# Threshold attention into a squared-ReLU MLP on one core: softmax reciprocals and divisions after the next step's maxima, one weight rounding moved a step, and the last weight block turned one step earlier

## The chip, the cores and the metric

The kernel runs as one launch on one core of a Trainium2 chip. The metric is the device time in microseconds (us), the median of several executions; the profile is of one further execution. The core has five queues that each run in program order: PE (matmuls; PEld is its weight loads), DVE (vector), ACT (scalar), POOL (GpSimd) and SP, which here only issues transfers. They meet through semaphores.

## The reference, cut to what matters

```python
# q, k, v: (8, 8, 576, 64) fp32; w_in (512, 2048), w_out (2048, 512); tau = 0.02
scores = q @ k.transpose(0, 1, 3, 2) / 8
thresh = scores.max(-1, keepdims=True) - tau
scores = np.where(scores >= thresh, scores, -1e9)
attn = np.exp(scores - scores.max(-1, keepdims=True))
attn = attn / (attn.sum(-1, keepdims=True) + 1e-9)
x = (attn @ v).transpose(0, 2, 1, 3).reshape(4608, 512)   # heads side by side
out = np.maximum(x @ w_in, 0) ** 2 @ w_out
```

## The kernel before

**Steps.** The attention is cut into 148 steps (`steps`, counted from 0; `NST` is 148, `END` is 150). A step is one block `i` of 128 query rows of one pair of heads (`vis`), and works on two heads `u` = 0, 1. The first four pairs have steps of two blocks each (steps 0 to 7), the next four of three blocks each (steps 8 to 19); the third block of those, `i` = 4, is a rest of 64 rows of both heads in one tile. A step consists of:

- *scores* on PE (L280, L273 for the rest), into four PSUM banks, two per head. The next step's scores reuse these banks, so they wait for L355 of the step before;
- *maxima* on DVE (L317), one per head;
- a bias and the exponentials on ACT (L331, L332, L335 in early steps; L340, L341, L343 later), into an SBUF tile `w`;
- *threshold* on DVE (L355): one scalar_tensor_tensor per head that compares the scores with the threshold, multiplies the exponentials by the result and leaves the row sum in `st`;
- a small reduction that bounds the sum from below and a *reciprocal* on DVE (L359, L360);
- *divide* on POOL (L365, then L367 per head): `w` times reciprocal;
- two steps later, `turn`: PE transposes `w` (L414, L421, L427) and ACT copies the result to `wT` (L415, L423, L428). From step 35 on DVE turns 32 x 32 blocks instead (`turn_blocks`, L459 to L469), and transfers place them: for each two blocks POOL issues one to DRAM (`set_aside`, L436, `aside`), and SP four from there into `wT` (L477);
- some steps after that, `mix`: PE multiplies `wT` by `v` (L530) and ACT copies the result to `xT` (L513 and its neighbours).

In between, DVE transposes the next keys and queries (`prep_part`, L254), and SP issues loads of q, k, v (L185, L188, L236).

**Early steps.** `early_to` is 11: steps 0 to 10 are written out by `early_step`. Steps 11 to 39 are in the main loop, steps 40 to 150 in `late_step`.

**Rounding of the MLP weights.** The weights arrive as 32 pieces (`weight_piece`), loaded by SP (L136) into three areas, and each is rounded in five stages by `round_weights(i, stage)`: stage 0 on ACT (L149, L150), stages 1 and 2 on DVE (L152, L154), stages 3 and 4 on POOL (L156, L158). `end_rounding` does stage 4, counts the piece in `state["rounded"]` and issues the load of the piece three further on. In the early steps a piece gets stage 0 in its own step (3, 5, 7, 8, 9) and the other stages in the next one: DVE's stages stand between L355 and L359, POOL's after the division. From step 11 on a piece has all its stages in its own step.

**MLP pieces.** When the first 256 tokens of `xT` are there, `add_chunk` puts the MLP's work into the queue `waiting`, in pieces of some 1.8 us of PE work (`PIECE_US`). `fill` takes pieces from it at four places of a step, at a rate that `rate` computes ahead. A piece may run if the number of rounded weight pieces that it needs is not over `state["usable"]`:

```python
state["usable"] = rounded_by[-1]          # the count at the start of the step before
rounded_by.append(state["rounded"])
```

The first chunk's first half is `mlp_in` (L579, four matmuls of 256 tokens, 8 PE instructions in the profile; relu and square by ACT L589 and DVE L591), its second half `mlp_out` (L764). `mlp_in` with `x` = 0 to 3 needs four rounded pieces. The first chunk is added in step 10. Later chunks use other products (L693, L799). All these decisions are made while the program is written down, so each queue's order is fixed.

**The end of the attention.** In `late_step` a step `s` turns the block of step `s` - 1. If that block's number is odd it does so right after its own maxima and exponentials (`first`), else behind its second `fill`. L816 is one of the additions that assemble the output of a chunk. Step 148 has no scores any more; it turns the block of step 147. The last `mix`, in step 150, needs what was turned, set aside and placed by then.

## Time and profile before

| What | us |
|---|---|
| median of three executions | 1318.65 (1318.54 to 1320.52) |
| the profiled execution | 1320.85 |
| its span, first to last instruction | 1319.1 |
| PE busy in the span | 1290.9 (98%) |
| DVE busy | 936.9 (71%) |
| POOL busy | 776.2 (59%) |
| ACT busy | 585.4 (44%) |

Three runs differ by up to 2.0 us, and the profiled one lies 2.2 us above their median. The page's busy time is a mean over parts that differ: up to about 200 us DVE is nearly as full as PE (9.8 of each 10 us from 70 to 110), later PE alone is full. PE's clock is granted at full speed almost everywhere (mean 0.997).

### The profile page before, as it was taken

The page shows a single profiled execution, that of the slowest core. Times are in us where ns is not written, and L with a number is a line of the kernel's source. Part 1 is how long each engine was busy: PE and PEld are TensorE (multiplying, and loading weights), DVE is VectorE, ACT ScalarE, POOL GpSimd, SP SyncE. Part 2 cuts the span into 40 slices and gives each one's busy share as a digit, 9 for nine tenths or more (in the row PEclk, how much of TensorE's full clock was granted, in tenths as well). Part 3 has the DMA queues.
Part 4 walks back from the last instruction along what each step waited for, and adds up shares of the span by engine and source line. Part 5 has one row for each costly group of instructions (what it writes and reads, how often), then busy time and mean ns, then how long its engine had stood idle before and what let it go on. Part 6 is the DMA issues. An engine that isn't in the chain of part 4 may idle for free.

```text
span 1319.1 us, 24730 instructions
## 1 busy us (share of the span) xinstructions
PE 1290.9 (98%) x8862; PEld 1070.6 (81%) x8862; DVE 936.9 (71%) x2034; ACT 585.4 (44%) x1353; POOL 776.2 (59%) x908
## 2 busy tenths in 40 slices
PE   7999999999999999999999999999999999999997
PEld 6676557897888888797978888888887988889997
DVE  6899776777777788788776877878686877522131
ACT  4887763244343526253435343525353434331331
POOL 3788874775747475556574746656574737455351
PEclk9999999999999999999999999999999999999999
DMA  6765431777777878686666768667676866520000
GB/s 127 156 181 145 126 73 60 145 173 168 165 173 178 181 177 186 143 200 160 170 157 158 158 154 187 172 137 185 146 173 139 198 162 161 144 53 9 9 17 17
DMA packets 320907, 185.48 MB, mean 141 GB/s; under 512 B 282224, under 2 KB 282256, under 8 KB 314384
## 3 DMA queue, kind: packets, MB, share of 16 engines
q1 hardware_dynamic: 309120, 115.78, 46.4%
q0 software_dynamic: 10000, 67.92, 12.9%
q8 instruction: 70, 1.15, 0.4%
q14 instruction: 53, 0.43, 0.1%
q10 hardware_dynamic: 1664, 0.21, 0.1%
HBM read 108.04 MB, written 68.42 MB: 134 GB/s over the span
## 4 chain that ended last, share of the span: by engine, by line
PE 83%; DVE 6%; DMA 3%; ACT 2%; issue 1%; POOL 1%; SPq 0%; DVEq 0%; POOLq 0%; ACTq 0%
PE big L693 29%; PE big L799 28%; PE big L530 10%; PE big L296 8%; PE big L579 3%; PE big L764 2%; PE big L280 2%; DVE st L317 1%; DMA wT<-aside 1%; DMA aside<-turned 1%; PE big L414 1%; DVE w L355 1%; ACT w L343 1%; DVE turned L154 0%; PE big L273 0%
## 5 line engine op out<-in xcount | busy, mean ns | idle before, releaser
L355 DVE SCALAR_TENSOR_TENSOR w<-big,st,w 128x576 f32<-128x576 f32 x269 | 207.4, 805 | 87.6 <-ACT w L343 85.6
L317 DVE TENSOR_REDUCE st<-big 128x1 f32<-128x576 f32 x288 | 204.1, 747 | 85.3 <-PE big L296 60.6
L367 POOL TENSOR_SCALAR w<-w,st 128x576 f32<-128x576 f32 x269 | 244.2, 916 | 29.4 <-DVE st L360 24.6
L799 PE MATMUL big<-wo,gsum 128*128 128x256 f32 x1088 | 243.8, 382 | 0.0
L799 PEld LDWEIGHTS big<-wo,gsum 128*128 128x128 f32 x1088 | 204.4, 190 | 37.0 <-issue 7.6
L693 PE MATMUL big<-xT,w_in_sb 128*128 128x128 f32 x1536 | 187.4, 277 | 1.5 <-DVE g L705 1.4
L693 PEld LDWEIGHTS big<-xT,w_in_sb 128*128 128x128 f32 x1536 | 178.5, 192 | 10.8 <-issue 7.7
L799 PE MATMUL big<-wo,g 128*128 128x256 f32 x816 | 185.3, 382 | 0.1
L343 ACT ACTIVATE w<-big,st 128x576 f32<-128x576 f32 x255 | 174.4, 735 | 0.2 <-issue 0.2
L799 PEld LDWEIGHTS big<-wo,g 128*128 128x128 f32 x816 | 151.6, 190 | 26.2 <-issue 6.5
L530 PE MATMUL big<-wT,vs 128*64 128x256 f32 (+5 forms) x1420 | 159.5, 389 | 4.9 <-DMA wT<-aside 3.5
L530 PEld LDWEIGHTS big<-wT,vs 128*64 128x64 f32 (+1 forms) x1420 | 86.0, 136 | 70.1 <-issue 20.8
L340 ACT ACTIVATE st<-st 128x2 f32<-128x2 f32 (+1 forms) x137 | 28.1, 205 | 253.3 <-DVE st L317 252.1
L365 POOL TENSOR_SCALAR st<-st 128x2 f32<-128x2 f32 (+1 forms) x148 | 35.6, 241 | 177.7 <-DVE w L355 167.1
L436 POOL DMA_DIRECT2D aside<-turned x50 | 29.9, 597 | 177.5 <-DVE turned L465 177.5
L705 DVE TENSOR_TENSOR g<-big,g 128x512 f32<-128x512 f32 x96 | 64.6, 676 | 83.7 <-PE big L693 78.1
L296 PE MATMUL big<-kT,qT 64*128 64x256 f32 (+3 forms) x768 | 107.0, 416 | 0.0
L296 PEld LDWEIGHTS big<-kT,qT 64*128 64x128 f32 x768 | 84.6, 186 | 14.5 <-issue 5.0
L701 ACT ACTIVATE g<-g 128x512 f32<-128x512 f32 x96 | 60.4, 630 | 63.5 <-DVE g L705 63.4
L569 POOL TENSOR_TENSOR gsum<-g 128x512 f32<-128x512 f32 x34 | 46.1, 1356 | 69.9 <-ACT g L702 69.6
L702 ACT ACTIVATE g<-g 128x512 f32<-128x512 f32 x128 | 80.9, 632 | 4.0
L459 DVE STREAM_TRANSPOSE turned<-w 128x512 f32<-128x512 f32 x100 | 70.2, 702 | 0.3 <-issue 0.3
(119 smaller groups left out, 2058.1 us busy)
## 6 DMA issues: line engine op xcount, KB each, us to landing
aside<-turned POOLq DMA_DIRECT2D x50, 1152.0 KB, 4.8
wT<-aside SPq DMA_DIRECT2D x200, 288.0 KB, 5.4
vs<-in_v_dram SPq DMA_DIRECT2D x72, 128.0 KB, 5.7
wo<-in_moe_w_in_dram SPq DMA_DIRECT2D x16, 512.0 KB, 4.8
wo<-in_moe_w_out_dram SPq DMA_DIRECT2D x16, 512.0 KB, 3.5
out_dram<-osb POOLq DMA_DIRECT2D x32, 256.0 KB, 3.9
kl<-in_k_dram SPq DMA_DIRECT2D x113, 72.0 KB, 2.8
ql<-in_q_dram SPq DMA_DIRECT2D x112, 72.0 KB, 5.7
```

Source lines behind the costliest of these rows:

```text
L296: nc.tensor.matmul(big[to, at + x0:at + x1], lhsT, keys[u * D:(u + 1) * D, x0:x1], start=True, stop=True)
L317: nc.vector.tensor_reduce(out=mx[:, u:u + 1], in_=sc[u], axis=AX.XY, op=ALU.max)
L343: nc.scalar.activation(out=w[:, u, :].rearrange("p (h k) -> p h k", h=2), in_=sc[u], func=AF.Exp, bias=bias[:, u:u + 1], scale=SCALE)
L355: nc.vector.scalar_tensor_tensor(out=wu, in0=sc[u], scalar=thr[:, u:u + 1], in1=wu, op0=ALU.is_ge, op1=ALU.mult, accum_out=sm[:, u:u + 1])
L367: nc.gpsimd.tensor_scalar(out=w[:, u, :], in0=w[:, u, :], scalar1=z[:, u:u + 1], scalar2=rcp[:, u:u + 1], op0=ALU.add, op1=ALU.mult)
L459: move(wb[:, 0:h, :, :], whole_[:, 0, :, :, :])
L530: nc.tensor.matmul(ps[u * D:(u + 1) * D, :], vs[n % 2][rows, u * (NBLK + 1) + c, :], wT[rows, at // REST:(at + ps.shape[1]) // REST, NBLK ...
L693: nc.tensor.matmul(to[:, f, :], factor(j, p, q, c)[:, f * P:(f + 1) * P], part[:, c, :], start=(p in "125" and f == 0 and c == 0), stop=(p ...
L701: nc.scalar.activation(out=to, in_=to if src is None else src, func=AF.Relu)
L702: nc.scalar.activation(out=to, in_=to, func=AF.Square)
L705: nc.vector.tensor_tensor(out=x, in0=to, in1=x, op=ALU.add)
L799: nc.tensor.matmul(to, left[:, f, :], wo[:, slot, f, :], start=(f == 0), stop=(f == HF - 1))
```

## The change

The reduction and the reciprocal become a function of their own, `reciprocals`. In the early steps from step 3 on `threshold` no longer calls it. The next step does, after its own maxima and exponentials: `finish_weights` issues the reciprocals, the division, and POOL's stages of the roundings whose DVE stages are done (kept in `turned_words`), with the loads that follow. Step 10 doesn't issue the DVE stages of the piece of step 9; step 11 does, after its maxima and after the reciprocal and the division of step 10. The DVE stages of step 11's own piece now both come after its threshold. In `late_step`, step 148 turns nothing more; step 147 turns the block of step 146 and then its own.

```diff
+    def reciprocals(vis, i):
+        st, n = weights[vis, i][2], len(weights[vis, i][1])
+        nc.vector.tensor_reduce(out=st[:, 5, 0:n], in_=st[:, 3:5, 0:n].rearrange("p j u -> p u j"), axis=AX.X, op=ALU.max)
+        nc.vector.reciprocal(st[:, 6, 0:n], st[:, 5, 0:n])
...
     def threshold(vis, i, between=()):
...
         for fn in between:
             fn()
-        nc.vector.tensor_reduce(out=den, in_=st[:, 3:5, 0:n].rearrange("p j u -> p u j"), axis=AX.X, op=ALU.max)
-        nc.vector.reciprocal(rcp, den)
+        if early() and state["step"] > 2:
+            return
+        reciprocals(vis, i)
...
     def late_step(s):
...
-        if first:
+        if first and s != NST:
             turn_last(s)
...
         if not first:
             some_later("vector")
             turn_last(s)
+            if s == NST - 1:
+                turn_last(NST)
...
+    def finish_weights(s):
+        reciprocals(*steps[s])
+        divide(*steps[s])
+        end_roundings()
+    def end_roundings():
+        while turned_words:
+            p = turned_words.popleft()
+            round_weights(p, 3)
+            end_rounding(p)
...
     def early_step(s):
...
         elif s > 2:
             scores(s)()
             early_exponents(n, i)
+        if s > 3:
+            finish_weights(s - 1)
...
-        threshold(n, i, [lambda p=p, x=x: round_weights(p, x) for p in rounding for x in (1, 2)])
-        divide(n, i)
-        while rounding:
-            p = rounding.popleft()
-            round_weights(p, 3)
-            end_rounding(p)
+        later_on = s == early_to - 1
+        threshold(n, i, [] if later_on else [lambda p=p, x=x: round_weights(p, x) for p in rounding for x in (1, 2)])
+        if not later_on:
+            turned_words.extend(rounding)
+            rounding.clear()
         rounding.extend(now)
+        if s < 3:
+            divide(n, i)
+            end_roundings()
...
     for s in range(END + 1):                      # the main loop, steps 11 to 39
...
             exponents(n, i)
+            if s == early_to:
+                finish_weights(s - 1)
+                while rounding:
+                    p = rounding.popleft()
+                    for x in (1, 2, 3):
+                        round_weights(p, x)
+                    end_rounding(p)
...
-            elif now:
+            elif now and s != early_to:
                 round_weights(now[0], 1)
...
-            if lay and now:
+            if now and (lay or s == early_to):
                 round_weights(now[0], 1)
```

## The prediction

> **What bounds the kernel now.** I read the page's engine rows, then the chain, then PE's idle times along the timeline, then the other engines at those places.

> ```profile
> PE 1290.9 (98%) x8862; PEld 1070.6 (81%) x8862; DVE 936.9 (71%) x2034; ACT 585.4 (44%) x1353; POOL 776.2 (59%) x908
> PE 83%; DVE 6%; DMA 3%; ACT 2%; issue 1%; POOL 1%; SPq 0%; DVEq 0%; POOLq 0%; ACTq 0%
> ```

> PE is busy 98% of the span. From about 60 us on its order runs nearly without holes, so the end moves only with PE's idle time after that, plus whatever the first 60 us gain or lose. Two stretches matter here.

> ```profile
> 34.26 0.82 DVE L355 SCALAR_TENSOR_TENSOR w<-big,st,w 128x576 f32<-128x576 f32 x1 [0.33 <-ACT st L331]
> 35.97 0.16 DVE L359 TENSOR_REDUCE st<-st 128x2 f32<-128x4 f32 x1
> 36.16 0.17 DVE L360 RECIPROCAL st<-st 128x2 f32<-128x2 f32 x1
> 36.41 1.61 DVE L317 TENSOR_REDUCE st<-big 128x1 f32<-128x576 f32 x2
> 37.94 0.77 DVE L254 STREAM_TRANSPOSE kT<-kl 128x576 f32<-128x576 f32 x1
> 38.70 0.82 DVE L355 SCALAR_TENSOR_TENSOR w<-big,st,w 128x576 f32<-128x576 f32 x1
> ...
> 58.96 1.24 PE L280 MATMUL big<-kT,qT 64*128 64x288 f32 x8 [1.76 <-DVE wo L355]
> 61.63 3.62 PE L579 MATMUL big<-xT,w_in_sb 128*128 128x256 f32 x16
> 65.18 1.24 PE L280 MATMUL big<-kT,qT 64*128 64x288 f32 x8
> ```

> (The timeline: start, length, engine, line, operation; in brackets the idle time before it and its releaser.) In the early steps DVE works almost without pause: two steps take 9.2 us, with 0.33 us lost to ACT. In step 11 (counted from 0) PE fills 61.63 to 65.25 with 16 instructions of L579, and the next scores follow at once. At the end of the attention part stands the last real PE hole:

> ```profile
> 1145.62 0.67 DVE L465 STREAM_TRANSPOSE turned<-w 128x512 f32<-128x512 f32 x1
> 1146.59 0.60 POOL L436 DMA_DIRECT2D aside<-turned  x1 [4.82 <-DVE turned L465]
> 1162.07 2.63 PE L530 MATMUL big<-wT,vs 128*64 128x256 f32 x24 [1.58 <-DMA wT<-aside]
> ```

> [...] L154 takes 0.43 us alone, but 1.39 us at 59.45, ending 0.28 us after POOL's L158 (59.21 to 60.56). [...] the granted clock is 0.51 from 18.0 to 21.5, and the 3.4 us before hold about 1.1 us of PE work.

> **The change part by part.** The number of instructions stays. I take the order of the built programs and walk it with the durations above.

> *Reciprocals and divisions moved (steps 3 to 10).* Reduction and reciprocal (L359, L360) cost 0.28 us of DVE issue (35.97 to 36.33, with the overlap into the next). They leave the place before the next maxima and come after them. In an odd step (5, 7) the maxima start 0.27 us earlier, because the roundings before them left the scores waiting; the pair then fills part of the 0.33 us that DVE waited for ACT: -0.27. In an even step (4, 6) no rounding stands before the maxima, so they already wait for PE (scores start 0.05 after L355 and need 1.23 us: 34.26 + 0.82 + 1.3 = 36.4, which is the start shown). Nothing is won there, while the pair now stands between maxima and the kT transpose, which led straight to L355 at 38.70: +0.28. Steps 8 and 9 start L355 when ACT is ready (ACT runs L149, L150 just before), so nothing moves. Sum to step 9: 0. Bounds: -0.8 if the even steps hide the pair, +0.9 if the odd steps gain nothing.

> [...] The division of step 8 now starts after the maxima of step 9, at 52.0 instead of 50.85, and POOL's roundings follow it: L156 at 53.6 to 54.9, L158 at 54.95 to 56.3 (before, 52.44 to 55.07). DVE's roundings of step 9 come at 54.45. Before they met only L158's tail (0.90 for L152). Now L152 meets L156 and L154 meets all of L158, ending near 56.6; the maxima of step 10 start at 56.5 instead of 56.00: +0.5. PE and ACT wait behind them. Bounds 0 and +1.3 (one whole L158).

> *Rounding of step 10's turn into step 11.* Its L152 and L154 (58.82 to 60.84) leave the place before the maxima of step 11, which then start about 60.7, when the scores are there, instead of 61.02. But reciprocal, L152 and L154 now precede L355[...]: L355 at 63.25 to 63.75 instead of 63.55. I take +0.1; bounds -0.3 to +0.2. SP: the loads L136 move behind loads of v and, in step 11, behind those of k and q; the piece needed at about 71 is issued near 64.5 and lands in 4.8 us (row of wo): no wait.

> *What the later rounding does to PE.* `rounded` is one piece behind (three instead of four when step 11 reads `usable`), so x = 0 of the first MLP chunk may not be placed in step 11. The built order shows it: step 11 loses both pieces (16 of L579), step 12 gets one more, step 16 the other. The order is equal again by step 17, apart from small shifts up to step 33. So PE stands idle in step 11 from about 62.3 to 65.1: a hole of 2.8 us, and the 3.46 us of work (16 x 0.216, their start distance) comes later. Step 12 repays 0.57 us (a hole before L427 in which the piece now lies), steps 13 and 16 0.22 and 0.75 (PE's waits for DVE at 76.1 and 93.5). Later holes of 1.03 and 0.62 (at 111.1 and 117.4) can repay more. Against that, pieces no longer lie between transposes in steps 17, 18, 20 and 21: there PE waits 0.41 or 0.57 for ACT's copies (as at 61.25 and 67.12), 1.96 if nothing covers it. DVE meets the POOL roundings 0.7 us later, too,[...]; that is the same delay seen from the other chain, not added. Hole 2.8 - 1.54 - 1.65 + 1.96 = +1.6[...]. Bounds: 0 (all repaid, no new waits) and +3.5.

> *Last block turned in its own step.* Four transposes (L459 to L465, 1144.75 to 1146.29) no longer stand behind L816, which waited for PE until 1144.41. They need the division (POOL L367 ends 1141.77), so they end at 1143.3, 2.9 us earlier, and POOL, idle 4.82 us, issues the aside transfer 2.9 us earlier. The four wT transfers of SP follow its landing; data is there at 1159.2 instead of 1162.07. PE wants it at 1160.48. L816 runs at its old time. So -1.6, all of the hole; bound on the other side 0.

> Sum: 0 + 0.5 + 0.1 + 2.2 - 1.6 = **+1.2 us**. The profiled execution took 1320.85 (span 1319.1 and 1.75 around it), 2.2 above the median of 1318.65; on the median that gives 1319.9.

> **The rivals.** *A, the likeliest:* the sum above, between 1318 and 1321.3. *B, slower:* the PE hole in step 11 makes the clock drop. [...] the hole leaves about 0.7 us, while the emptiest such stretch of before near 57 holds 1.6 and shows full clock. Half clock for 3.4 us costs 1.7 us of PE work, and PE is then too late to be repaid: 2.8 + 0.5 + 1.7 - 1.6 = +3.4, 1322.1[...]. [...] *C, faster:* later DVE waits repay the hole (2.8 + 0.4 against 0.57 + 0.22 + 0.75 + 1.03 + 0.62 = 3.2), [...]the even steps hide the pair: -0.8 - 1.6 = -2.4, 1316.2. Against it: DVE and PE are both full in steps 12 to 21 (9.7 of 10 us in 70 to 110). *D, the turn does not do what it says:* the aside transfer took 7.7 us in that place, and if it ends no earlier the gain is lost: +2.8, 1321.4. POOL's idle time speaks against it.

> **How the numbers follow.** A 0.55, B 0.25, C 0.14, D 0.06. A measurement of this kernel can tell about 0.2% (2.6 us) from no change: below 1316.0 is faster, above 1321.3 slower. Half of C lies below (0.08); B and half of D with the edge of A above (0.29); 0.63 within. Range 1316.0 to 1323.4; A alone 1318 to 1321.3.

> **What would show it.** Right: no L579 in step 11 and a PE wait for L355 of 2 to 3 us before the scores of step 12; L152 or L154 near 1 us or more in step 9; maxima of step 10 about 0.5 us later; no PE wait for wT<-aside near 1160. Granted clock below 1 near 65 to 69 means B. Scores of step 17 no later than 93.5 would mean C; a remaining wait at 1160 means D. If step 10's maxima come before 55.7, my walk of the early steps is wrong.

## The result, and the profile after

| | before | after |
|---|---|---|
| median of the executions, us | 1320.04 (5 executions) | 1325.73 (5 executions) |
| profiled execution, us | 1320.85 | 1326.58 |
| its span, us | 1319.1 | 1324.8 |
| mean granted PE clock in the span | 0.997 | 0.995 |

The ratio after to before is 1.0049, interval 1.0033 to 1.0065: **slower, by 5.7 us between the medians** and by 6.5 us (4.4 to 8.6) as the ratio has it. The forecast was 1319.9 with a range up to 1323.4.

The engine rows and the chain of the kernel after, as on its page:

```profile
PE 1293.2 (98%) x8862; PEld 1071.9 (81%) x8862; DVE 933.6 (70%) x2034; ACT 583.8 (44%) x1353; POOL 776.0 (59%) x908
PE 83%; DVE 4%; DMA 4%; ACT 3%; issue 1%; POOL 1%; SPq 0%; DVEq 0%; POOLq 0%; ACTq 0%
```

The same number of instructions on each engine, and PE is busy 2.3 us longer (1293.2 against 1290.9). The order of PE's products doesn't change how much there is to multiply, so some instructions took longer: a first sign of the clock (mean 0.995 against 0.997). The timeline of the kernel after, first DVE in steps 5 and 6 and, with one line of POOL, at the end of step 9, then PE in steps 11 and 12, then the end of the attention (start, length, engine, line; in brackets the idle time before, and its releaser; lines from L349 on stand a few lower or higher than before: L355 is L361, L359 and L360 are L349 and L350, L579 is L586, L414 is L421, L415 is L422, L436 is L443, L465 is L472, L530 is L537; runs made from the kernel before keep its numbers):

```profile
34.88 0.82 DVE L361 SCALAR_TENSOR_TENSOR w<-big,st,w 128x576 f32<-128x576 f32 x1
36.19 1.60 DVE L317 TENSOR_REDUCE st<-big 128x1 f32<-128x576 f32 x2 [0.48 <-PE big L280]
37.70 0.15 DVE L349 TENSOR_REDUCE st<-st 128x2 f32<-128x4 f32 x1
37.88 0.17 DVE L350 RECIPROCAL st<-st 128x2 f32<-128x2 f32 x1
38.16 0.78 DVE L254 STREAM_TRANSPOSE kT<-kl 128x576 f32<-128x576 f32 x1
38.86 0.78 DVE L361 SCALAR_TENSOR_TENSOR w<-big,st,w 128x576 f32<-128x576 f32 x1
...
54.15 0.90 DVE L152 TENSOR_SCALAR turned<-turned 128x512 uint32<-128x512 uint32 x1
54.85 1.34 POOL L158 TENSOR_TENSOR w_in_sb<-turned 128x512 f32<-128x512 f32 x1
55.09 1.39 DVE L154 TENSOR_SCALAR turned<-turned 128x512 uint32<-128x512 uint32 x1
56.40 0.74 DVE L317 TENSOR_REDUCE st<-big 128x1 f32<-128x576 f32 x1
...
59.37 1.24 PE L280 MATMUL big<-kT,qT 64*128 64x288 f32 x8 [2.46 <-DVE wo L361]
60.54 0.88 PE L421 MATMUL big<-ident,w 128*128 128x128 f32 x6
62.97 0.55 PE L421 MATMUL big<-ident,w 128*128 128x128 f32 x3 [1.55 <-ACT wT L422]
65.20 2.54 PE L280 MATMUL big<-kT,qT 64*128 64x288 f32 x7 [1.68 <-DVE w L361]
...
68.57 3.55 PE L586 MATMUL big<-xT,w_in_sb 128*128 128x256 f32 x8
...
1149.10 0.67 DVE L472 STREAM_TRANSPOSE turned<-w 128x512 f32<-128x512 f32 x1
1150.07 0.60 POOL L443 DMA_DIRECT2D aside<-turned  x1 [1.41 <-DVE turned L472]
1167.83 2.63 PE L537 MATMUL big<-wT,vs 128*64 128x256 f32 x24 [0.45 <-DMA wT<-aside]
```

What to see. The maxima of step 6 (36.19) still wait for PE, now in the trace's own words, and the pair of reduction and reciprocal (L349, L350) stands between them and the kT transpose, as forecast. At 55.09 L154 takes 1.39 instead of 0.43 us and ends 0.29 us after POOL's L158, which ran beside it; L152 ahead of it takes 0.90 instead of 0.42 and ends 0.28 us after POOL's L156 (53.49 to 54.77). In before L152 takes 0.90 there and ends 0.28 us after L158 (53.79 to 55.07). The traces show this pattern, and not what makes it. In step 11 no L586 stands between 63.5 and 65.2: PE has holes of 1.55 and 1.68 us, where it was full before. And the instructions behind the hole are slow: 8 of L586 take 3.55 us, where 16 took 3.62 in the kernel before; 7 of L280 take 2.54, where 8 took 1.24. That is half speed: 0.44 us for one of L586 against 0.23, at a granted clock of 0.50 from 64.93 to 71.76 us. At the end of the attention POOL is idle for 1.41 us before the last set-aside (4.82 before), and PE still waits 0.45 us for wT (1.58 before).

The table by stage says the same in the clock column. It has start and end of the stretch, its length, busy time (and instructions) of PE, PEld, DVE, ACT and POOL, then the granted clock, the DMA share and GB/s. The kernel after:

```profile
58.00:62.00 4.00, 2.05 (x14) 1.32 (x14) 2.19 (x5) 2.34 (x8) 3.83 (x5) 1.00 1.05 236
62.00:65.00 3.00, 0.55 (x3) 0.31 (x3) 2.23 (x6) 2.99 (x9) 2.19 (x3) 0.99 0.46 59
65.00:68.00 3.00, 2.80 (x12) 2.30 (x13) 2.52 (x9) 1.94 (x4) 2.03 (x3) 0.50 0.79 153
68.00:72.00 4.00, 4.00 (x13) 2.96 (x11) 3.18 (x10) 3.50 (x8) 3.81 (x5) 0.53 1.05 306
72.00:76.00 4.00, 4.00 (x22) 3.47 (x22) 2.79 (x5) 1.86 (x4) 2.96 (x5) 1.00 0.62 198
```

and the kernel before in two of these stretches:

```profile
62.00:65.00 3.00, 3.00 (x16) 2.51 (x14) 3.00 (x5) 2.51 (x7) 2.69 (x3) 1.00 0.46 62
68.00:72.00 4.00, 4.00 (x20) 3.38 (x19) 3.74 (x11) 4.00 (x10) 3.36 (x4) 1.00 0.76 218
```

At 0.50 the clock was low for twice the missing share: 2 x (3.00 x 0.01 + 3.00 x 0.50 + 4.00 x 0.47) = 6.8 us. Up to the maxima of step 12 (67.52) the kernel after is only 1.06 us late; at those of step 13 it is 4.12 us late, 6.5 at those of step 18, 6.9 to 7.4 from 172 us to the last scores, and 5.7 at the end. So most of the loss arises between the maxima of steps 12 and 13, where the clock is low, and the rest in the steps behind them, and the forecast's rival B (1322.1, where the range went up to 1323.4) is what happened, at a higher price. Three things were open: is the count of usable pieces behind it, is it the half clock or the hole, and do the moved DVE work, the moved loads and the tail have a part.

### The profile page after: what moved, and what is told of

It reads as the page before. It is cut to its first block, busy times and chain, and to the rows that moved or that the text cites. A ratio compares the mean times of both kernels' runs of the same rounds, so it can differ in the third digit from the quotient of the medians.

```text
span 1324.8 us, 24737 instructions
## 1 busy us (share of the span) xinstructions
PE 1293.2 (98%) x8862; PEld 1071.9 (81%) x8862; DVE 933.6 (70%) x2034; ACT 583.8 (44%) x1353; POOL 776.0 (59%) x908
## 4 chain that ended last, share of the span: by engine, by line
PE 83%; DVE 4%; DMA 4%; ACT 3%; issue 1%; POOL 1%; SPq 0%; DVEq 0%; POOLq 0%; ACTq 0%
PE big L700 29%; PE big L806 27%; PE big L537 10%; PE big L296 8%; PE big L586 4%; PE big L280 2%; PE big L771 2%; DMA aside<-turned 2%; DMA wT<-aside 1%; DVE st L317 1%; PE big L421 1%; DVE w L361 1%; ACT w L343 1%; ACT wT L422 0%; DMA wo<-in_moe_w_in_dram 0%
## 5 line engine op out<-in xcount | busy, mean ns | idle before, releaser
L361 DVE SCALAR_TENSOR_TENSOR w<-big,st,w 128x576 f32<-128x576 f32 x269 | 207.6, 807 | 89.5 <-ACT w L343 88.0
L317 DVE TENSOR_REDUCE st<-big 128x1 f32<-128x576 f32 x288 | 204.4, 748 | 92.7 <-PE big L296 60.5
L537 PE MATMUL big<-wT,vs 128*64 128x256 f32 (+5 forms) x1420 | 159.5, 389 | 4.9 <-DMA wT<-aside 2.6
L537 PEld LDWEIGHTS big<-wT,vs 128*64 128x64 f32 (+1 forms) x1420 | 85.9, 136 | 70.4 <-issue 19.0
L443 POOL DMA_DIRECT2D aside<-turned x50 | 29.9, 598 | 173.8 <-DVE turned L472 169.5
```

The lines of the kernel that those rows point to most:

```text
L317: nc.vector.tensor_reduce(out=mx[:, u:u + 1], in_=sc[u], axis=AX.XY, op=ALU.max)
L361: nc.vector.scalar_tensor_tensor(out=wu, in0=sc[u], scalar=thr[:, u:u + 1], in1=wu, op0=ALU.is_ge, op1=ALU.mult, accum_out=sm[:, u:u + 1])
L537: nc.tensor.matmul(ps[u * D:(u + 1) * D, :], vs[n % 2][rows, u * (NBLK + 1) + c, :], wT[rows, at // REST:(at + ps.shape[1]) // REST, NBLK ...
```

## The experiments

The twelve runs below are compared by ratio with the kernel before of their own group; 0.1% is 1.32 us. The medians of before in the three groups were 1320.56, 1320.6 and 1320.98, and 1320.02 beside the last run. A difference between two runs of different groups is rougher than its decimals.

### The late count alone, and the change without it

`late_count` is the kernel before with one edit; DVE's order, the loads and the tail stay.

```diff
-        state["usable"] = rounded_by[-1]
+        state["usable"] = 3 if s == early_to else rounded_by[-1]
```

> The kernel before, with the count that step 11 reads set to three rounded pieces instead of four, so that its two MLP pieces go to steps 12 and 16 as in the changed kernel; the order of DVE, the loads and the tail stay as before. Theory 1 (clock): the hole in step 11, about 2.7 us in one piece, makes PE's clock drop in most executions: +3 to +5 us, granted clock 0.5 for 3.4 or 6.8 us near 65. Theory 2 (only idle time, the clock by chance): +1 to +2.5 us. Theory 3 (the late load of a weight piece made the loss): the load is on time here, so under +1 us.

Measured: 1326.44 us, ratio 1.0042 (1.0030 to 1.0055), which is +5.5 us (4.0 to 7.3), as much as the whole change loses. Of the three theories only the first (+3 to +5) meets that interval. Its stages show a milder form of the same drop:

```profile
62.00:65.00 3.00, 1.28 (x6) 0.79 (x8) 2.93 (x8) 2.94 (x8) 1.98 (x2) 0.98 0.68 79
65.00:68.00 3.00, 3.00 (x15) 2.28 (x13) 1.97 (x4) 2.09 (x6) 2.55 (x4) 0.50 0.71 123
68.00:72.00 4.00, 4.00 (x21) 3.17 (x21) 3.67 (x9) 2.36 (x6) 3.37 (x4) 0.96 0.94 263
```

Then the other way round: `pieces_back` is the kernel after with the count of before in step 11. The roundings stay where the change puts them.

```diff
-        state["usable"] = rounded_by[-1]
+        state["usable"] = state["rounded"] if s == early_to else rounded_by[-1]
```

> The kernel after, but the count of usable pieces that step 11 reads is the one of the kernel before (the roundings themselves stay where the change puts them), so that the two pieces of L586 lie in step 11 again. Theory 1 (the late count is the whole loss: hole, clock drop and repayment that never comes): no PE wait of 2 us in step 11, clock 1.0 at 64 to 70, 4.5 to 6 us less than after, so -0.5 to +1.5 us against before (the DVE moves of the early steps +0.4, the tail -1.1, one later load). Rival (the DVE moves of the early steps and the late load cost 2 us or more of their own): +2 to +3.5 against before.

Measured: 1320.56 us, ratio 1.0004 (0.9996 to 1.0012): 5.2 us below after and level with before. Its PE timeline has the 16 instructions of L586 back in step 11:

```profile
63.05 0.55 PE L421 MATMUL big<-ident,w 128*128 128x128 f32 x3 [1.49 <-ACT wT L422]
63.43 3.62 PE L586 MATMUL big<-xT,w_in_sb 128*128 128x256 f32 x16
66.98 1.24 PE L280 MATMUL big<-kT,qT 64*128 64x288 f32 x8
```

The count is thus both enough for the loss and needed for it. The hole of 1.49 us before the last transposes is still there, but `loads_pieces` below, whose trace has 0.24 us in that place, is no faster beyond the noise (0.9998 against 1.0004).

### Half clock or hole

`clock_kept` is the kernel after, and `late_clock` is `late_count`, each with matmuls on unused data in step 11's hole: `keep_busy(12, 7)` issues 12 transposes of the identity into PSUM bank 7.

```diff
             turn(*old, 1)()
+            if s == early_to:
+                keep_busy(12, 7)
...
             turn(*old, 2)()
+            if s == early_to:
+                keep_busy(13, 7)
```

> The changed kernel with 25 transposes of the identity put into PE's holes of step 11 (12 before the last three transposes of the weights, 13 after them); nobody reads what they write. Theory 1 (clock): the granted clock stays at 1.0 near 65, and the half-speed work of 6.8 us is done in 3.4: -3.4 us against the changed kernel, +2.3 against before. Theory 2 (idle time alone): the same time as the changed kernel, +5.7 against before. Theory 3 (late load): no gain either, ACT waits as long for the piece.

> The kernel before with the late count alone (three pieces instead of four at step 11) and matmuls on unused data in step 11's hole (12 after the first third of the transposes, 13 after the second), so that the clock has no reason to drop. The count alone took +5.9 us against before with the clock at half for 3.4 us near 65. Theory (the half clock is a bit under half of that, 2 to 3 us, the rest is the hole that isn't repaid): +3 to +4 against before, clock 1.0 at 62 to 70. Rival 1 (the clock drop is nearly all of it): +0 to +1.5. Rival 2 (the drop is covered by PE's other waits): +5 to +6 with the clock at 1.0.

Measured: `clock_kept` 1322.73, ratio 1.0015 (1.0009 to 1.0022); `late_clock` 1323.17, ratio 1.0016 (1.0008 to 1.0024). The stages of `clock_kept`, and one of `late_clock` as the last line:

```profile
62.00:65.00 3.00, 3.00 (x30) 3.00 (x29) 2.93 (x7) 2.87 (x8) 2.10 (x4) 1.00 0.73 74
65.00:68.00 3.00, 3.00 (x23) 2.05 (x21) 2.90 (x9) 2.37 (x5) 2.19 (x2) 1.00 0.75 146
68.00:72.00 4.00, 4.00 (x22) 3.24 (x21) 3.27 (x8) 2.63 (x6) 3.66 (x5) 1.00 1.06 302
65.00:68.00 3.00, 3.00 (x22) 2.39 (x22) 2.53 (x8) 2.47 (x8) 1.82 (x3) 1.00 0.94 232
```

The filler computes nothing that is used, and adds PE work; yet it takes 3.0 us off the kernel after and 3.3 off the late count (medians; by the ratios 4.5 and 3.4). What it removes is the low clock (1.00 from 62 to 72 us, where after had 0.50 to 0.53 and `late_count` 0.50 in 65 to 68). It doesn't move the work around it: the scores of step 12 start 5.47 us after those of step 11 in `late_clock`, and 5.46 us in `late_count`. The rest of the late count, with the clock whole, is 0.0016 x 1320.6 = 2.1 us (1.1 to 3.2): the hole that isn't repaid. That lies between the theory of `late_clock` (+3 to +4) and its rival 1 (0 to +1.5), so the half clock is a bit more than half of the loss; rival 2, that the drop costs nothing, falls. `clock_kept` came as its first theory had it.

The mean clocks of the executions fit this, roughly. In `clock_kept` 17 of 21 have 0.998; the one at 1325.67 us, the slowest, has 0.993, and the next, at 1324.5, 0.995. The five executions of after have 0.993 to 0.997, at 1325.4 to 1328.9. The mean can't do more: it is rounded to 0.001, which is 1.3 us, and it holds the drop near 18 us too. The executions of after at 1325.35 and 1325.39 have 0.997 and 0.995. The proof is in the two runs with the filled hole.

### The moved loads

The end of a rounding also issues the load three pieces on, so it moves with it. In the kernel after, ACT waits for one of them in step 11:

```profile
61.34 0.66 ACT L149 ACTIVATE turned<-wo 128x512 f32<-128x512 f32 x1 [1.66 <-DMA wo<-in_moe_w_in_dram]
```

Behind it ACT copies wT (L422, 62.46), and for that PE waited 1.55 us. `loads_back` is the kernel after with the loads at the place where before issues them; `loads_clock` has matmuls on unused data besides (4 and 22 instead of 12 and 13); `loads_pieces` has these loads and the count of before, so that only DVE's order and the tail are left of the change.

```diff
+    def load_next(p):
+        if p + RAW < n_pieces:
+            loaded.add(p + RAW)
+            load_weights(p + RAW)
...
-        if p + RAW < n_pieces:
+        if p + RAW < n_pieces and p + RAW not in loaded:
...
+        for p in rounding:
+            load_next(p)
         threshold(n, i, ...)
```

> The changed kernel with the loads of the weight pieces issued where the kernel before issues them on SP; all else as changed. Theory 3 (late load): ACT's wait of 1.66 us before L149 near 61.3 is gone, with it PE's wait of 1.55 us at 62.97, and the clock no longer drops: -4 us or more against the changed kernel. Theory 1 (clock): the hole behind the transposes of step 11 becomes one of 2.7 us, the clock still drops: -0.5 to -1.5 us. Theory 2: -1.5 us.

> The kernel after with the loads of the early steps issued where before issues them, and matmuls on unused data in step 11's hole (4 and 22). With the filled hole alone the kernel after took +2.1 us against before and -3.0 against after. Theory (the late load costs a little only when the clock is whole): +1 to +2 against before. Rival (load is hidden): +2.1 as without it. If the clock drops all the same: +4 or more, with a granted clock below 0.9 somewhere from 58 to 74.

> The kernel after with the count of before and with the loads of the early steps issued where before issues them: what stays is the order of DVE's work in steps 3 to 11 and the tail. Theory (moved DVE work is worth +0.4 as at the maxima of step 10, the tail -1.1): -0.7 us against before, between -1.5 and +0.5; against pieces_back 0 to -1. Rival (DVE's later roundings delay PE in step 11[...]): +1 to +2 against before, with a PE wait for DVE of over 1 us in steps 11 to 13.

Measured: `loads_back` 1326.02 (ratio 1.0043, 1.0031 to 1.0056), `loads_clock` 1323.77 (1.0024, 1.0015 to 1.0033), `loads_pieces` 1320.29 (0.9998, 0.9990 to 1.0006). Each stands within 1.1 us of its partner with late loads (1325.73, 1322.73, 1320.56), so the late load is no measurable part of the loss. None of the three gains that were expected of `loads_back` came. The theory behind `loads_clock`, that the load would show once the clock is whole, falls: +3.2 us (2.0 to 4.4) is above its +1 to +2. Three of the ten executions of `loads_clock` have a mean clock of 0.995, so its filler may not have kept the clock in all of them. In the profiled execution of `loads_back`, without the wait for the load, the clock fell earlier, and for longer; it is the slowest of the five (1328.3 us, median 1326.02).

```profile
58.00:62.00 4.00, 1.66 (x8) 1.19 (x8) 1.69 (x6) 3.53 (x9) 3.34 (x4) 0.73 0.97 280
62.00:65.00 3.00, 2.94 (x13) 1.64 (x9) 2.27 (x6) 1.34 (x5) 1.47 (x3) 0.50 0.60 73
65.00:68.00 3.00, 1.48 (x5) 1.24 (x7) 2.93 (x8) 2.94 (x7) 2.49 (x3) 0.50 0.80 165
68.00:72.00 4.00, 4.00 (x19) 3.24 (x16) 3.25 (x6) 2.51 (x7) 2.92 (x5) 0.50 0.82 220
72.00:76.00 4.00, 4.00 (x18) 2.89 (x18) 3.83 (x9) 1.64 (x5) 3.22 (x3) 0.81 0.39 110
```

### The DVE moves and the tail by themselves

`moves_only` is `loads_pieces` without the tail edit. `tail_only` is the kernel before with the tail edit alone:

```diff
-        if first:
+        if first and s != NST:
             turn_last(s)
...
             turn_last(s)
+            if s == NST - 1:
+                turn_last(NST)
```

> DVE's moves of the early steps alone: the kernel after with the count and the loads of before, and the tail of before. With the tail it took -0.3 us against before, and the tail alone -1.1. Theory ([...]): +0.5 against before, between 0 and +1. Rival (the moves cost more[...]): +1.5 or more. Rival 2 (they bring a gain): below 0.

> The kernel before with the last edit alone: step 147 turns its own block, nothing else moves. Every theory of the early part expects the same here: the PE wait of 1.58 us for wT<-aside near 1162 is gone, so -1.5 us against before (-1.3 to -1.6). Rival (the transfer ends no earlier): 0 us, the wait still there.

Measured: `moves_only` 1321.63, ratio 1.0008 (1.0002 to 1.0015), +1.1 us (0.3 to 2.0); `tail_only` 1319.45, ratio 0.9993 (0.9987 to 1.0000), -0.9 us (-1.7 to 0). In the traces of these two, the maxima of step 4 start 0.08 us earlier in `moves_only`, those of step 8 0.33 us later, those of step 10, behind the roundings of step 9, 1.00, those of step 13 1.72, and the last ones 1.21. So, against step 8, the roundings of step 9 cost about 0.7 us. Another 0.7 come in steps 11 and 12, where the roundings have other places too, and 0.4 in step 4, where the kT transpose waits 0.51 us; which of the moves in steps 11 and 12 it is was not tried. The interval of the ratio holds the theory's +0.5, the rival's +1.5 and the 1.3 us that the traces show up to the last maxima.

The moves do one more thing: before the scores of step 11 PE waits 2.46 us instead of 1.76. Executions with a mean clock of 0.995 or less occur in `moves_only` (3 of 21), `loads_pieces` and `pieces_back` (2 of 13 each), and in none of before, `tail_only` and `late_clock`, where the roundings are not moved; `mended_start`, which lacks the drop at the start, has two of 13 at 0.996. A drop near 60 us in a part of the executions would explain them; `mended_start` below has one in its trace. No such execution of the three was profiled, so this stays open.

In the tail the edit does what it says: POOL's idle time before the last set-aside is 1.42 us instead of 4.82, and PE no longer waits for wT. `tail_only`:

```profile
1144.33 0.60 POOL L436 DMA_DIRECT2D aside<-turned  x1 [1.42 <-DVE turned L465]
1159.27 4.79 PE L530 MATMUL big<-wT,vs 128*64 128x320 f32 x40
```

But the profiled execution of `moves_only`, which has the tail of before, shows no such wait either:

```profile
1148.95 0.60 POOL L443 DMA_DIRECT2D aside<-turned  x1 [4.83 <-DVE turned L472]
1160.47 4.87 PE L537 MATMUL big<-wT,vs 128*64 128x320 f32 x40
```

All 40 instructions run on without a break. There the transfer landed 6.1 us after its issue, against 7.7 in before's trace. Of the four traces with this tail, before has a hole of 1.58 us, `late_count` of 1.45, `late_clock` of 1.11, and `moves_only` none: it is not always there, and the edit can only remove what is there. The interval of `tail_only` just reaches 0.

### A version below both

The clock of before falls in 18 to 21.5 us too (0.50 from 18.06 to 21.47). `tail_start` puts 14 matmuls on unused data into PE's idle stretch ahead of it, on top of the tail edit; `mended_start` does so in `loads_pieces`. Their matmuls write over part of step 1's scores, so only their times are read. `tail_start2` writes to columns 384 to 511 of the bank, which hold no scores.

```diff
             scores(2)()
+            for x in range(14):
+                nc.tensor.transpose(bank[7][:, 3 * P:4 * P], ident, ident)
             early_exponents(*steps[2])
```

> The kernel before with the tail edit and 14 matmuls on unused data after step 2's scores (issued in step 1), where PE idles at about 15 to 17 us and the clock stands at half from 18 to 21.5. The tail alone took -1.1 us against before. Theory (an idle stretch of PE sets the clock drop, and half clock costs where PE has a full order): clock 1.0 at 16 to 24 and -1.5 to -2.5 us against before. Rival 1 (DVE sets the first 60 us): clock 1.0 but no more than the tail, -1.1. Rival 2: the drop comes at another place (granted clock below 0.9 from 8 to 26), -1 or more.

> The kernel after with the count and the loads of before and the same 14 matmuls. Without them -0.3 us against before, though its trace shows the clock low at 16 to 20. Theory: clock 1.0 at 16 to 24, -0.8 to -2 against before. Rival (DVE sets the first 60 us): -0.3 as without.

> The kernel before with the tail edit and the 14 matmuls on unused data after step 2's scores, now in the columns of a bank that hold no scores (the first form wrote over scores of step 1; its time was 2.3 us below before, by 0.14%). Theory: the same time, -1.5 to -2.8 us against before, clock 1.0 at 16 to 24. Rival: the writes into a bank that DVE is reading cost something of their own: -1 or less.

Measured: `tail_start` 1318.65, ratio 0.9986 (0.9979 to 0.9992); `tail_start2` 1318.24, ratio 0.9991 (0.9984 to 0.9997), -1.2 us (-2.1 to -0.4); `mended_start` 1320.19, ratio 0.9995 (0.9987 to 1.0003). `mended_start` can't tell its theory from its rival. `tail_start` came as its theory had it (-1.8 us); `tail_start2`, which was to repeat it, lies between its theory (-1.5 to -2.8) and its rival (-1 or less). `tail_start2` is below both kernels. Whether the filler adds to the tail edit stays open: the intervals of both runs overlap with that of `tail_only`. That the clock stays whole there is seen in its stages:

```profile
16.00:18.00 2.00, 1.45 (x13) 1.45 (x14) 1.28 (x3) 1.94 (x6) 0.00 (x0) 1.00 0.68 135
18.00:20.00 2.00, 1.34 (x12) 1.10 (x11) 1.34 (x5) 1.02 (x3) 0.35 (x2) 1.00 0.84 270
20.00:22.00 2.00, 2.00 (x17) 1.72 (x16) 2.00 (x5) 0.73 (x2) 1.50 (x2) 1.00 1.02 408
```

`mended_start` shows why its gain is less sure: with the start's drop gone, its profiled execution has one near 60 us instead.

```profile
56.00:58.00 2.00, 1.00 (x20) 0.76 (x14) 1.96 (x5) 0.64 (x2) 0.86 (x3) 1.00 1.08 294
58.00:60.00 2.00, 0.53 (x2) 0.40 (x4) 0.85 (x3) 2.00 (x7) 2.00 (x3) 0.90 0.92 253
60.00:62.00 2.00, 2.00 (x10) 1.09 (x7) 0.31 (x1) 0.91 (x2) 1.84 (x2) 0.50 1.09 332
```

## Why the prediction was wrong, and where it was right

**The step that failed: the half clock behind PE's hole stands in the sum as nothing.** The prediction saw the hole, saw that it leaves less PE work in 3.4 us than the stretch before the drop at 18 us, and still gave the drop 0.25. The place and the length of the drop differ from trace to trace (65 to 72 in after, from 59.8 on in `loads_back`, 65 to 68.3 in `late_count`); in all three traces that have the hole there is one. Its measured price is 3.0 us (after against `clock_kept`) or 3.3 (`late_count` against `late_clock`).

**Rival B was closer than its total shows.** It had +4.5 us for hole and clock together (2.8 + 1.7), and `late_count`, which has only these two, measured +5.5 (4.0 to 7.3). B's total of +3.4 is short of the measured 5.7 by 2.3: 1.0 there, 0.6 at the moved DVE work and 0.7 at the tail. Its "half clock for 3.4 us" took the length from the drop at 18 us in before's trace (3.41 us); after's lasted 6.8 us. Trace against trace, aligned at the first maxima and read at the last, `late_count` loses 2.4 us on `late_clock` with a drop of 3.4 us, and after 3.7 us on `clock_kept` with one of 6.8.

**The base was low, too.** The forecast started from 1318.65, the median of three executions of before. With two more the median is 1320.04, and in the later groups 1320.02 to 1320.98. This moved the forecast's absolute time down by 1.4 to 2.3 us, and does not touch its difference of +1.2.

The other terms of the sum, against what the runs showed:

| step of the prediction | said, us | measured, us | by |
|---|---|---|---|
| reciprocals and divisions moved, to step 9 | 0 | +0.1 (maxima of step 4 0.61 us early, of steps 5 to 8 0.23 to 0.26, of step 9 0.55) | after's trace |
| DVE's roundings beside POOL's in step 9, roundings of step 10 | +0.6 | +1.1 (0.3 to 2.0), with the row above | `moves_only` |
| PE's hole and its repayment | +2.2 | +2.1 (1.1 to 3.2) | `late_clock` |
| last block turned in its own step | -1.6 | -0.9 (-1.7 to 0) | `tail_only` |
| sum with the clock whole | +1.2 | +2.0 (1.2 to 2.9) | `clock_kept` |
| half clock | not in the sum | +3.0 (medians), +4.5 (ratios) | after less `clock_kept` |

- **The early steps** were right in kind: even steps wait for PE, and L152 and L154 met POOL at 0.90 and 1.39 us, as worked out. "L154 meets all of L158" came true to 0.1 us (ending 56.48, said near 56.6).
- **The hole** was right in its cause and its place; the trace has it in two parts, 1.55 and 1.68 us. That its net cost came out at +2.1 is luck in part: the terms gave +1.6, and the +2.2 adds 0.6 for DVE's later meeting with POOL's roundings, the author's estimate of a delay that the text had just called "not added". None of the repayments was measured by itself. The loads' "no wait" was wrong: the prediction looked at the piece needed at about 71 us and missed the one needed at 61, where ACT waited 1.66 us. It had no measurable price.
- **The tail** was right in direction and too large, since the 1.58 us of one execution were taken as if they were in every one. The sign "no PE wait" did not quite come: 0.45 us are left in after.
- Rivals C and D fell. Scores weren't early, and the wait at the end shrank.

The stretch ahead of a drop was not idle: its last 3.41 us held 0.55 to 1.62 us of PE work (figures in the last section). And stretches that hold about as much don't all end in one: `pieces_back` has 1.06 and 0.49 us of PE work in 56 to 58 and 58 to 60 and keeps its clock (1.00 in both); `mended_start`, with 1.00 and 0.53, loses it (0.90, then 0.50). What decides between the two was not shown. Such a stretch should have been priced as a drop that comes in a part of the executions, and the emptier one in step 11 as one that comes in most: both are the author's estimates, the second from the three traces that have that hole.

## What to carry to other kernels

Before work is moved, follow what its place is counted by: here a rounding that ended a step later made a planner withhold two pieces of PE work, and that alone cost as much as the whole change lost. Where PE is full, price a hole of 2 to 3 us in two parts, its own length less what later waits repay, and the half clock behind it; here the second part was the larger (3.0 to 3.3 us by the medians, against 2.1). And read a stall from more than one execution before an edit's gain is set to its full length.

## What the runs showed of the hardware

```profile
61.52:64.93 3.41, 0.55 (x3) 0.31 (x3) 2.65 (x6) 3.41 (x9) 2.51 (x4) 1.00 0.60 66
56.21:59.62 3.41, 0.94 (x18) 0.70 (x14) 2.60 (x7) 2.26 (x7) 2.27 (x5) 1.00 1.02 269
56.50:59.91 3.41, 0.95 (x12) 0.66 (x10) 2.21 (x6) 2.42 (x7) 2.36 (x4) 1.00 0.85 245
```

The clock fell behind stretches with 0.55, 0.94, 1.18 (`late_count`), 1.44 (`loads_back`) and, at the start, 0.96 (before) to 1.62 us of PE work (`moves_only`); it held with 0.95 (after), 1.56 (`moves_only`, 56.92 to 60.33) and 1.57 (`clock_kept`, 56.20 to 59.61). So in these traces neither the longest wait nor the PE work of such a stretch tells by itself whether the clock falls.
- Matmuls on unused data cost less than they saved, though PE is busy 98% of the span: 25 of them in step 11 brought 3.0 us (`clock_kept` 1322.73 against 1325.73).
